# Lightning attention and a SiLU feed-forward on one core: half of block 4's first product in seven products, another order of the opening, other transfer times in the planner

## The chip, the cores and the metric

One core of a Trainium2 chip. The metric is device time in microseconds (us) of one launch, on the slowest (here the only) core. The engines are PE (TensorE, matrix products), ACT (ScalarE), DVE (VectorE), POOL (GpSimd) and SP (SyncE), which here only issues transfers. Each engine runs its own instructions in the order of the program; between engines there are semaphores.

## The reference

Attention in blocks of 64 positions with a decay per head, for 4 batches, 8 heads, 768 positions, 64 wide; then a feed-forward layer over the 3072 tokens of width 512, with 2048 hidden features.

```python
for b in range(nb):                       # 12 blocks of 64
    qb, kb, vb = (q[:, :, sl], k[:, :, sl], v[:, :, sl])
    intra = np.einsum('bhic,bhjc->bhij', qb, kb) * Dmask[None]
    intra = np.einsum('bhij,bhjd->bhid', intra, vb)
    inter = np.einsum('bhid,bhde->bhie', qb * lam_pow[None], kv_state)
    out[:, :, sl] = intra + inter
    kb_dec = kb * rev_pow[None]
    kv_state = lam_block[None, :, None, None] * kv_state + np.einsum('bhsd,bhse->bhde', kb_dec, vb)
...
h = x @ w_in                              # x: (3072, 512), w_in: (512, 2048)
g = h * (1.0 / (1.0 + np.exp(-h)))
return (g @ w_out).astype(np.float32)     # w_out: (2048, 512)
```

Inputs and output are float32. The kernel multiplies in bfloat16 and sums in float32.

## The kernel before

**Units and sets.** A unit is 128 positions of one batch (24 units). Two units form a set, for which q, k and v are loaded together (512 KB each): sets 0 to 3 hold the first two units of one batch each ("paired", `prepare_2`, `first_2`, `second_2`), sets 4 to 11 hold the same unit of two batches. The feed-forward works on eight groups: groups 0 to 3 of 256 tokens (a paired set each) and groups 4 to 7 of 512 tokens (two sets each). Blocks here are numbered by unit: block 4 is group 6, the last but one, and group 7 is the last.

**Attention of a set.** The names are those of the tiles in the profile. `kq`: keys cast to bfloat16 (ACT or DVE) and queries scaled by powers of the decay (DVE). `tr`: PE transposes of `kq`, copied to `kqT`; from set 5 on a DMA does this. `vd`: scaled values. `st_ps` holds the scores, masked by DVE into `st`. `d_ps` holds the products of keys and values, from which DVE makes the running states `y`, `xf` (float32) and ACT or POOL the block-diagonal bfloat16 copies `xe`. `x_ps` gets the two products `vd` x `st` (`outs`) and state x queries (`inter`), and is copied to `xt`, the transposed input of the feed-forward.

**Feed-forward.** `product1` multiplies `xt` by `w_in`: four products for each `h_ps` result, then SiLU on ACT into `g`. In a group of 512 tokens it has 16 results of 4 products with 512 columns. For group 7, `product1_spared` does this in seven products in place of eight (Strassen's scheme in Winograd's form): sums of the quarters of `w_in` (`S1` to `S4`, tile `wsum`) and of `xt` (`T1` to `T4`, tile `xsum`) are made by DVE, and in four parts (`jp`) two PSUM banks `P` and `R` take the seven products, with copies (`m`, `h_ps`) and sums (`h`) by ACT and DVE between them. The second product, by `w_out` into `o_ps`, is plain for the first eight units (`product2_plain`, four steps of four products with 512 columns, a quarter of `w_out` each) and in seven products for the rest (`product2`, `products_of`, with sums `s`).

**Order.** Nothing runs in the order in which it is written. Each piece of work is a `Task` with a key, the engines that may do it with an estimated cost, what it depends on, and the buffers that it takes from counted pools. `Planner.order` goes through time with these costs and a model of the transfers (`SMALL`, `WIDE`, `LARGE`, `HALF` and others: bytes of a packet and two times; `FIRST`: time from issue to first packet), gives each free engine the ready task with the smallest key, and so fixes for each engine one order, in which the program is then written. Its times have no part in the run; on the chip only the order and the semaphores count. Where PE has nothing to do in the first 24 us of the plan, dummy products (`ones`) are put in.

**Transfers.** Loads of q, k and v are issued by SP, weights by POOL, results by ACT and at the end by SP. `SEQUENCE` gives the order of the loads; a mark such as `@1.2` makes the issuing engine wait until an earlier load has landed, by a copy to `gate` of one element of it:

```python
SEQUENCE = "s0 i0@0.2 s1 i1a@0.2 i1b i2 i3 o0 o1 s2@1.2 o2 o3 s3 s4"
```

So set 2's loads wait for set 1's values, and the third and fourth quarter of `w_out` (`o2`, `o3`) for set 2's keys. Sets 0 to 3 load queries, keys, values in this order.

**Lines of the profile.** L513 and L693 `tr`; L588 and L737 scores; L534 and L727 states; L614, L619, L759, L767 `x_ps`; L905 `product1`, L917 its SiLU; L1023 the seven products of the last group, L1047 their SiLU; L940 plain second product, L1153 that in seven; L1236 dummies; L342 and L344 copies by ACT and DVE; L349 every DVE operation with two tensors; L360 gates of POOL; L380 and L385 loads by SP; L406 and L409 weights.

Of the kernel before, what the change touches and what calls it, by code (L numbers as in the profile page):

```python
# [33 lines left out]

SMALL, WIDE, CAST, LARGE, HALF, TURN = (256, 17.5, 20.0), (512, 25.0, 28.0), (256, 14.0, 31.0), (2048, 88.0, 90.0), (1024, 58.0, 58.0), (1024, 50.0, 50.0)


class Planner:
# [5 lines left out]
    BIAS = {"DVE": 0.2}  # L44
    SLOW, SLOWER = 15.5, 1.8
    DENSE, THIN, REST = (9.6, 17.0), 24.0, 0.3
    FIRST, LAST, AHEAD = {"SP": 1.9, "ACT": 1.15, "POOL": 2.5}, 1.0, 0.75

# [168 lines left out]
def kernel(  # L217
# [30 lines left out]
                 xt2=2, xt4=2, g=18, s=12, m=3, osb=3, one=3, two=8, att=6, sp=2)  # L248
    BY_POOL, IN_BY_POOL, PLAIN, SPARED = (), (), 8, 1
    CASTING, SUMS_AFTER, HURRY, SUMS_ON, HOLD, ONTO = 12, 16, 0.0, 9.0, 1, 24  # L250
    EARLY, PACE = 1.0, 1.0
    OPEN, FILLED, SCALED = 4, True, ()
    QUERIES = (0, 1, 2, 3)
    SCORED, SOON, VD_ON, HALVED = (0, 1), 3, {"DVE": 0.7}, 0
    EAGER, CALM, ON = 8.0, 1.0, 6.0
# [92 lines left out]
    def tt(e, o, a, b, op):  # L348
        (nc.vector if e == "DVE" else nc.gpsimd).tensor_tensor(o, a, b, op=op)  # L349


    gate = const.tile([128, 16], F32, name="gate")
# [49 lines left out]
    def load_w(key, what, j, part):  # L402
        def go(e):
            if what == "i":
                cs = {"": slice(512 * j, 512 * j + 512), "a": slice(512 * j, 512 * j + 256), "b": slice(512 * j + 256, 512 * j + 512)}[part]
                nc.gpsimd.dma_start(out=w_in_bf[:, :, cs], in_=w_in_r[:, :, cs])  # L406
            else:
                ks = slice(4 * j, 4 * j + 4)
                nc.gpsimd.dma_start(out=w_out_bf[:, ks, :], in_=w_out_r[:, ks, :])  # L409

        t = pool_task(add((key, 0), {"POOL": 0.8}, go, [], [], 0.5243 if part else 1.0486,
                          HALF if part else LARGE, prior=pool_last[-1:], late=1.0))
        wload.setdefault((what, j), []).append(t)
        for h in ("a", "b") if not part else part:
            wload[what, j, h] = t
# [64 lines left out]
    def prepare_2(o, rs, lk, lq, lv):  # L480
# [5 lines left out]
        def cast(e, i, a):  # L486
            src = rs[i].tile[:, :, a, :].rearrange("p (m h) d -> p m h d", h=2)
            if i:
                rate = lam_q2[:, :, a].rearrange("p (m h) -> p m h", h=2)
                tt(e, o.kq_of()[:, i, :, a], src, rate[:, :, :, None].to_broadcast([128, NP, 2, 64]), AL.mult)  # L490
            else:
                copy(e, o.kq_of()[:, i, :, a], src)

        o.ck = [[add((s - (2.95 if i and o.si in SCALED else 1.0), i), {"DVE": 0.7} if i else {"DVE": 0.45, "ACT": 0.63}, lambda e, i=i, a=a: cast(e, i, a),
                     deps=(lk, lq)[i], bufs=[rs[i], o.kq]) for a in range(2)] for i in range(2)]
        after("k", [t for ts in o.ck for t in ts])

        def scale_v(e, a):
            hs = slice(4 * a, 4 * a + 4)
            tt(e, o.vd_of()[:, hs].rearrange("p h e d -> p (h e) d"), rs[2].tile[:, hs].rearrange("p h e d -> p (h e) d"),  # L500
               lam_v2[:, hs].rearrange("p h e -> p (h e)")[:, :, None].to_broadcast([128, 8, 64]), AL.mult)

        o.cv = [add((s - 0.8, 0), VD_ON, lambda e, a=a: scale_v(e, a), deps=lv, bufs=[rs[2], o.vd]) for a in range(2)]
        after("v", o.cv)
# [18 lines left out]
    def first_2(o):  # L523
# [42 lines left out]
        def rest():  # L566
            td = add((s - 0.6, 0), {"PE": 0.45}, states, deps=o.cv + o.ck[0], bufs=d_ps + [o.kq, o.vd])
            after("b", td)
            t0 = add((s - 0.9, SOON), {"DVE": 0.42}, lambda e: tt(e, small(xf), d_ps[0].tile, rate, AL.mult), deps=[td], bufs=[d_ps[0], xf])
            o.xe_ready = blocks(o.xe_in, 0, lambda: xf.tile, t0, xf)  # L570
            t1 = add((s - 0.9, 4), {"DVE": 0.42}, lambda e: tt(e, small(y), d_ps[1].tile, xf.tile, AL.add), deps=[td, t0],
                     bufs=[d_ps[1], xf, y])
            t2 = add((s - 0.9, 5), {"DVE": 0.42}, lambda e: tt(e, xf_of(), y.tile, rate, AL.mult), deps=[t1], bufs=[y, xf_n])
            xf_t.append(t2)
            xe_t.extend(blocks(xe_n, b0 % 2, xf_of, t2, xf_n))

        if o.si not in SCORED:
            rest()
        deps = [t for t in o.turned]
        o.masked = []  # L580
        for g in range(2):
# [8 lines left out]

            ts = add((s - 0.5, g), {"PE": 0.4}, scores, deps=deps, bufs=st_ps[g] + [o.kqT])
            after("b", ts)
# [41 lines left out]
    def prepare(si):  # L634
# [28 lines left out]
        def cast(e, j, i):  # L663
            src = rs[i].tile[:, j * H:j * H + H, :]
            dst = kq_of()[:, i, j].rearrange("p m h d -> p (m h) d")
            if i:
                tt(e, dst, src, lam_q[:, :, None].to_broadcast([128, H, 64]), AL.mult)
            else:
                copy(e, dst, src)

        ck = [[add((s - 1.0, i), {"DVE": 0.7} if i else {"DVE": 0.45, "ACT": 0.63}, lambda e, j=j, i=i: cast(e, j, i),
                   deps=(lk, lq)[i], bufs=[rs[i], o.kq]) for i in range(2)] for j in range(nb)]
        if si < CASTING:
            after("k", [t for ts in ck for t in ts])

        def scale_v(e, j):
            tt(e, vd_of()[:, j], rs[2].tile[:, j * H:j * H + H, :], lam_v[:, :, None].to_broadcast([128, H, 64]), AL.mult)

        cv = [add((s - 0.8, 0), VD_ON, lambda e, j=j: scale_v(e, j),
                  deps=lv, bufs=[rs[2], o.vd]) for j in range(nb)]  # L680
# [206 lines left out]

    def product1(gi):

# [3 lines left out]
        mine = []  # L893
        for m0 in range(0, KO, 2 * per):
            g = Buf("g")
# [58 lines left out]
    W = {}  # L954
# [9 lines left out]
    def sums_of_w_in():  # L964
        bufs = {name: Buf("kq") if i else Buf("rb") for i, name in enumerate(("S1", "S2", "S3", "S4"))}
        for name, b in bufs.items():
            W[name] = lambda b=b: tile_of(b, [128, 2, 1024], BF16, "wsum")
        loads = [t for i in range(4) for t in wload["i", i]]
        done = {"A11": loads, "A12": loads, "A22": loads}

        every = [t for o in infos if rank[o.n, o.bs[0]] < SUMS_AFTER for t in o.cv] + [t for o in infos[:CASTING] for ts in o.ck for t in ts]

        def total(name, a, b, op, deps, on):
            done[name] = [add((on, 8), {"POOL": 2.4} if name in IN_BY_POOL else {"DVE": 0.7}, lambda e, ks=ks: tt(
                e, W[name]()[:, ks], W[a]()[:, ks], W[b]()[:, ks], op), deps=deps, bufs=[bufs[name]])
                          for ks in (0, 1)]

        on = SUMS_ON
        total("S1", "A21", "A22", AL.add, loads + every, on)
        total("S2", "S1", "A11", AL.subtract, done["S1"], on + 0.1)  # L980
        total("S3", "A11", "A21", AL.subtract, loads + every, on + 0.2)
        total("S4", "A12", "S2", AL.subtract, done["S2"], on + 0.3)
        return bufs, done

    def product1_spared(gi, wbufs, wdone):

# [4 lines left out]
        def X(name):  # L991
            i, r = {"B11": (0, lo), "B12": (0, hi), "B21": (1, lo), "B22": (1, hi), "T1": (0, hi)}.get(name, (0, lo))
            if name in ("T2", "T4"):
                return tile_of(two, [128, 2, 2, 256], BF16, "xsum")[:, int(name == "T4")]
            if name == "T3":
                return tile_of(one, [128, 2, 256], BF16, "xsum")
            return x.tile[:, 2 * i:2 * i + 2, r]
# [7 lines left out]
        total("T2", "T3", "B11", AL.add, done["T3"], [one, two])  # L1005
        total("T1", "B12", "B11", AL.subtract, done["T3"], [])
        total("T4", "B21", "T2", AL.subtract, done["T2"], [two])
        for jp in range(4):
            P, R = Buf("bank"), Buf("bank")
            held = [P, R, Buf("sp")]  # L1010
            low, high = Buf("g"), Buf("g")
# [22 lines left out]

            narrow = {"22": Buf("vd"), "12": Buf("st")}

# [19 lines left out]
            m6 = product(2, P, "S2", "T2", False, [c1])  # L1056
            b2, c2 = keep("kqT", [m6])
            m5 = product(3, R, "S1", "T1", True, [s11])
            m7 = product(4, P, "S3", "T3", False, [c2])
            b3, c3 = keep("xf", [m7])  # L1060
            e22 = total_of("22", b3, [m5, c3])
# [148 lines left out]

    for gi in range(len(groups) - SPARED):
        product1(gi)
    for t in waits:
        t.deps += gs[0, 0][2]
        t.bufs.append(gs[0, 0][0])
        gs[0, 0][0].left += 1
    if SPARED:
        made = sums_of_w_in()
        for gi in range(len(groups) - SPARED, len(groups)):
            product1_spared(gi, *made)  # L1220
    by_rank = sorted(rank, key=rank.get)
# [51 lines left out]
```

## Time and profile before

| What | Value |
|---|---|
| Median of 3 runs (lowest to highest) | 204.62 us (204.29 to 204.93) |
| The profiled execution: its own time | 204.46 us |
| Its span, first to last instruction | 202.4 us |
| Mean granted clock of PE | 0.997 |
| Busy: PE, DVE, ACT, POOL | 188.1, 135.5, 114.2, 21.8 us |
| DMA | 33.40 MB, mean 165 GB/s |
| PE products of L905 (512 columns; 256 columns) | 184 and 256 records |
| PE products of L1023 | 112 records |

The page gives busy time by engine, the span in 40 slices of 5.06 us with the busy share in tenths, and the chain of work that ended last, followed back from the end. The timeline lists instructions in order of time, like ones merged; "[idle before <-releaser]" is the idle time of the engine ahead of the instruction and what ended it. Matmuls are pipelined: the length of one record holds its latency, so that the pace of a row of them is read from start to start, or from the lengths in the chain.

### The profile page before, as it was taken

To read this page: it belongs to the slowest core of one execution; us is meant where nothing else is said; L and a number is where in the kernel's file an instruction comes from. 1 tells how busy PE (TensorE), PEld (TensorE's weight loads), DVE (VectorE), ACT (ScalarE), POOL (GpSimd) and SP (SyncE) were. 2 spreads that over 40 slices of the span, in tenths; PEclk is the share of its full clock that TensorE was granted. 3 is DMA by queue.
4 is the path that set the end of the run, shared out by engine and by line. 5 is a ranking of instruction groups with operands and counts; after the bars stand their busy time and mean duration, and the time that the engine had idled before them with its cause. 6 is when DMAs were issued, how large, how long until landed. Compare 5 with 4: busy or idle time off the path is not lost.

```text
span 202.4 us, 5779 instructions
## 1 busy us (share of the span) xinstructions
PE 188.1 (93%) x2494; PEld 135.0 (67%) x2512; DVE 135.5 (67%) x269; ACT 114.2 (56%) x207; POOL 21.8 (11%) x48
## 2 busy tenths in 40 slices
PE   0588999999999999999999999999999999999992
PEld 0476788557678655544488746486676778888881
DVE  6499620595997950969999774999577553646511
ACT  3836666327567642357764394945656575685320
POOL 6093100310110100001011000110200000000000
PEclk9999999999999999999999999999999999999998
DMA  3999999999999989999999999948001111003313
GB/s 94 301 274 202 216 215 250 254 193 212 239 269 242 206 204 261 174 267 212 202 142 231 253 194 222 225 104 160 2 3 55 52 52 36 19 0 107 104 50 108
DMA packets 87067, 33.40 MB, mean 165 GB/s; under 512 B 65026, under 2 KB 86018, under 8 KB 87042
## 3 DMA queue, kind: packets, MB, share of 16 engines
q1 hardware_dynamic: 77154, 23.07, 57.0%
q0 software_dynamic: 4752, 4.19, 12.9%
q10 hardware_dynamic: 5136, 5.77, 8.9%
q8 instruction: 19, 0.31, 0.7%
q14 instruction: 6, 0.05, 0.1%
HBM read 27.27 MB, written 6.29 MB: 166 GB/s over the span
## 4 chain that ended last, share of the span: by engine, by line
PE 84%; DVE 6%; DMA 4%; ACT 3%; issue 1%; DVEq 0%; SPq 0%
PE h_ps L905 33%; PE o_ps L1153 22%; PE o_ps L940 14%; PE h_ps L1023 6%; DMA raw<-in_k_dram 3%; DVE st L349 2%; PE x_ps L767 2%; PE d_ps L727 1%; PE tr L513 1%; PE x_ps L759 1%; DVE vd L349 1%; PE st_ps L737 1%; DMA out_dram<-osb 1%; ACT xt L342 1%; DVE kqT L344 1%
## 5 line engine op out<-in xcount | busy, mean ns | idle before, releaser
L905 PE MATMUL h_ps<-xt,w_in_bf 128*128 128x256 bf16 (+1 forms) x440 | 73.7, 317 | 0.7 <-ACT xt L342 0.3
L905 PEld LDWEIGHTS <-w_in_bf 128*128 128x128 bf16 x448 | 42.9, 98 | 24.9 <-issue 0.3
L917 ACT ACTIVATE g<-h_ps 128x512 bf16<-128x512 f32 x80 | 46.8, 595 | 20.9 <-PE h_ps L905 20.3
L940 PE MATMUL o_ps<-w_out_bf,g 128*128 128x512 bf16 x118 | 28.6, 379 | 0.8 <-issue 0.5
L1153 PEld LDWEIGHTS <-g 128*128 128x128 bf16 x256 | 25.0, 98 | 3.7
L349 DVE TENSOR_TENSOR st<-st_ps,tri 128x512 bf16<-128x512 f32 x32 | 20.3, 682 | 9.3 <-PE st_ps L737 9.3
L1153 PEld LDWEIGHTS <-s 128*128 128x128 bf16 x192 | 18.7, 98 | 2.8
L349 DVE TENSOR_TENSOR kq<-raw,lam_q 128x512 bf16<-128x512 f32 x24 | 16.3, 698 | 6.2 <-DMA raw<-in_q_dram 4.5
L940 PEld LDWEIGHTS <-g 128*128 128x128 bf16 x128 | 12.0, 98 | 12.0
L349 DVE TENSOR_TENSOR osb<-o_ps,m 128x512 f32<-128x512 f32 (+1 forms) x15 | 8.6, 581 | 13.4 <-ACT m L342 8.6
L342 ACT ACTIVATE xt<-x_ps 128x512 bf16<-128x512 f32 x16 | 9.7, 631 | 12.3 <-PE x_ps L767 9.2
L349 DVE TENSOR_TENSOR vd<-raw,lam_v 128x512 bf16<-128x512 f32 x24 | 15.7, 682 | 0.7 <-DMA raw<-in_v_dram 0.7
L1153 PE MATMUL o_ps<-w_out_bf,s 128*128 128x256 bf16 x128 | 15.3, 273 | 0.0
L1153 PE MATMUL o_ps<-wsum,g 128*128 128x256 bf16 x128 | 15.1, 273 | 0.0
L1153 PE MATMUL o_ps<-w_out_bf,g 128*128 128x256 bf16 x128 | 14.8, 273 | 0.0
L342 ACT ACTIVATE osb<-o_ps 128x512 f32<-128x512 f32 (+1 forms) x13 | 7.3, 564 | 12.7 <-PE o_ps L940 8.6
L349 DVE TENSOR_TENSOR s<-g 128x512 bf16<-128x512 bf16 x16 | 7.2, 447 | 10.8 <-ACT g L917 8.1
L342 ACT ACTIVATE m<-o_ps 128x512 f32<-128x512 f32 (+1 forms) x13 | 6.7, 515 | 13.1 <-PE o_ps L1153 12.9
L513 PE MATMUL tr<-ident,kq 128*128 128x128 bf16 x64 | 6.1, 241 | 7.7 <-DVE kq L349 7.5
L342 ACT ACTIVATE kq<-raw 128x512 bf16<-128x512 f32 x14 | 8.4, 624 | 4.5 <-DMA raw<-in_k_dram 4.0
L346 POOL CAST xe<-xf 64x256 bf16<-64x256 f32 (+1 forms) x8 | 5.1, 640 | 49.4 <-DVE xf L349 39.3
L513 PEld LDWEIGHTS <-kq 128*128 128x128 bf16 x64 | 4.6, 107 | 8.4 <-DVE kq L349 7.9
(90 smaller groups left out, 225.0 us busy)
## 6 DMA issues: line engine op xcount, KB each, us to landing
raw<-in_q_dram SPq DMA_DIRECT2D x12, 512.0 KB, 8.2
raw<-in_k_dram SPq DMA_DIRECT2D x12, 512.0 KB, 7.9
raw<-in_v_dram SPq DMA_DIRECT2D x12, 512.0 KB, 7.2
out_dram<-osb ACTq DMA_DIRECT2D x20, 256.0 KB, 4.2
w_out_bf<-in_moe_w_out_dram POOLq DMA_DIRECT2D x4, 512.0 KB, 14.9
w_in_bf<-in_moe_w_in_dram POOLq DMA_DIRECT2D x3, 512.0 KB, 11.7
w_in_bf<-in_moe_w_in_dram POOLq DMA_DIRECT2D x2, 256.0 KB, 8.2
out_dram<-osb ACTq DMA_DIRECT2D x4, 128.0 KB, 1.7
```

The source lines that it names most:

```text
L342: nc.scalar.activation(o, i, AF.Copy)
L344: nc.vector.tensor_copy(o, i)
L346: nc.gpsimd.tensor_copy(o, i)
L349: (nc.vector if e == "DVE" else nc.gpsimd).tensor_tensor(o, a, b, op=op)
L513: nc.tensor.transpose(t[:, m, a], o.kq_of()[:, i, m, a], ident)
L727: nc.tensor.matmul(d_of(c)[rp, j, m, :], lhsT=o.kq_of()[r, 0, j, m, p, :], rhs=o.vd_of()[r, j, 2 * m + p, :], start=j == 0 and m == 0, sto ...
L767: nc.tensor.matmul(x_of(c)[:, j, m, :], lhsT=o.xe[c].tile[:, (bs[0] + j) % 2, m, :], rhs=o.kqT_of()[:, 1, j, m, halves[c]], start=False, s ...
L905: nc.tensor.matmul(t[:, j, :], lhsT=w_in_bf[:, ko, 128 * (m1 + j):128 * (m1 + j) + 128], rhs=xt[gi].tile[:, ko, :], start=(ko == 0), stop= ...
L917: nc.scalar.activation(t[:, half * per:half * per + per], bank.tile, AF.Silu)
L940: nc.tensor.matmul(t, lhsT=g.tile[:, j, 128 * gp:128 * gp + 128], rhs=w_out_bf[:, ko, :], start=(ko == 0), stop=(ko == KO - 1))
L1023: nc.tensor.matmul(t[:, j, :], lhsT=W[w]()[:, k2, f:f + 128], rhs=X(r)[:, k2, :], start=first and j == 0 and k2 == 0, stop=True, skip_grou ...
L1153: nc.tensor.matmul(t[:, i_, :], lhsT=src(j)[:, k2, 128 * r:128 * r + 128], rhs=W[w]()[:, 2 * j + k2, :], start=first and i_ == 0 and j == ...
```

## The change

It has five parts.

- **Planner.** Other constants for the transfers (`LARGE`, a new class `PART` for the halved weight loads, `FIRST` for SP and POOL) and for PE's slow start (`SLOW`).
- **Opening.** `SCALED = (1,)`: set 1's query scaling gets a key 1.95 smaller. `FINE`: in the plan, the scores of each pair of heads depend on the two `kqT` copies of these heads alone, not on all four. `LAZY = 2.0`: the last state step of a paired set (`xf`) gets the key `s + 2.0` in place of `s - 0.9`.
- **Group 6 (block 4).** `MIXED = (0, 1)`: parts 0 and 1 of its first product, half of the results, go through `product1_spared`; the other half stays in `product1`, which takes a list of results for it. The scratch buffers for group 6 come from the pools `y`, `kq` and `yf`; `T1` gets a place of its own and no longer overwrites a part of `xt`.
- **Sums of `w_in`.** They no longer depend in the plan on all casts and value scalings (`every`), but follow SP's last load, and `S3` follows the last casts; three of them lie in `rb` buffers.
- **Places for other engines** (`by_act`, `by_rate`, `ON_ACT`). `ON_ACT` is empty, so nothing comes of them.

The order that the program then has, on PE from the first transposes of set 2 on: before, 88 products of groups 0 and 1 in all, `tr` x8 (queries), 32 products, 8 `o_ps`, 8 products, `tr` x8 (keys), 12 `o_ps`, states; after, 64 products, `tr` x8 (queries), 56 products, `tr` x8 (keys), 8 `o_ps`, 8 products, 8 `o_ps`, states. On SP and POOL the loads stand in the same order through set 3.

```diff
-SMALL, WIDE, CAST, LARGE, HALF, TURN = ..., (2048, 88.0, 90.0), (1024, 58.0, 58.0), (1024, 50.0, 50.0)
+SMALL, WIDE, CAST, LARGE, HALF, TURN, PART = ..., (2048, 86.0, 86.0), (1024, 58.0, 58.0), (1024, 50.0, 50.0), (1024, 45.0, 45.0)
...
-    SLOW, SLOWER = 15.5, 1.8
+    SLOW, SLOWER = 14.0, 1.8
...
-    FIRST, LAST, AHEAD = {"SP": 1.9, "ACT": 1.15, "POOL": 2.5}, 1.0, 0.75
+    FIRST, LAST, AHEAD = {"SP": 1.7, "ACT": 1.15, "POOL": 3.0}, 1.0, 0.75
...
-    OPEN, FILLED, SCALED = 4, True, ()
+    OPEN, FILLED, SCALED = 4, True, (1,)
...
+    LAZY, FINE = 2.0, True
+    MIXED, APART, KEPT = (0, 1), 1, "yf"
...
-                          HALF if part else LARGE, prior=pool_last[-1:], late=1.0))
+                          PART if part else LARGE, prior=pool_last[-1:], late=1.0))
...
-            t2 = add((s - 0.9, 5), {"DVE": 0.42}, lambda e: tt(e, xf_of(), y.tile, rate, AL.mult), deps=[t1], bufs=[y, xf_n])
+            t2 = add((s + LAZY, 5), {"DVE": 0.42}, lambda e: tt(e, xf_of(), y.tile, rate, AL.mult), deps=[t1], bufs=[y, xf_n])
...
-            ts = add((s - 0.5, g), {"PE": 0.4}, scores, deps=deps, bufs=st_ps[g] + [o.kqT])
+            ts = add((s - 0.5, g), {"PE": 0.4}, scores, deps=o.turned[g::2] if FINE else o.turned, bufs=st_ps[g] + [o.kqT])
...
-        for m0 in range(0, KO, 2 * per):
+        for m0 in tiles or range(0, KO, 2 * per):
...
-        bufs = {name: Buf("kq") if i else Buf("rb") for i, name in enumerate(("S1", "S2", "S3", "S4"))}
+        bufs = {name: Buf("kq" if name == "S3" else "rb") for name in ("S1", "S2", "S3", "S4")}
...
-        total("S1", "A21", "A22", AL.add, loads + every, on)
+        total("S1", "A21", "A22", AL.add, loads, on)
         total("S2", "S1", "A11", AL.subtract, done["S1"], on + 0.1)
-        total("S3", "A11", "A21", AL.subtract, loads + every, on + 0.2)
+        total("S3", "A11", "A21", AL.subtract, casts, on + 0.2)
...
-            narrow = {"22": Buf("vd"), "12": Buf("st")}
+            narrow = {"22": Buf("vd" if closing else "y"), "12": Buf("st" if closing else "y")}
...
-    for gi in range(len(groups) - SPARED):
+    for gi in range(len(groups) - 2):
         product1(gi)
...
+    made = sums_of_w_in()
+    left = [j for j in range(4) if j not in MIXED]
+    if left:
+        product1(len(groups) - 2, [m for j in left for m in (2 * j, 2 * j + 8)])
+    if MIXED:
+        product1_spared(len(groups) - 2, *made, MIXED)
+    product1_spared(len(groups) - 1, *made, range(4))
```

## The prediction

> **What bounds it now.** I read the page first (busy time, slices), then the chain of waits, then the timeline of the opening, then busy time by stage.
>
> ```profile
> PE 188.1 (93%) x2494; PEld 135.0 (67%) x2512; DVE 135.5 (67%) x269; ACT 114.2 (56%) x207; POOL 21.8 (11%) x48
> ...
> PE   0588999999999999999999999999999999999992
> ...
> DMA  3999999999999989999999999948001111003313
> ```
>
> TensorE (PE) is full from the fourth slice (about 20 us) to the end, and the DMA engines are full from the second slice to about 135 us. So the time is the moment at which PE becomes full, plus its work, plus any hole. The chain of waits says where that moment is, and what PE then does (columns: start, length, what):
>
> ```profile
> 24.32 0.04 issue
> 24.36 6.28 PE h_ps L905 x56
> 30.64 0.45 PE tr L513 x8
> 31.09 3.49 PE h_ps L905 x32
> 34.58 0.21 PE o_ps L940
> 34.79 0.05 issue
> 34.85 1.46 PE o_ps L940 x6
> 36.30 0.87 PE h_ps L905 x8
> 37.18 0.45 PE tr L513 x8
> 37.62 2.59 PE o_ps L940 x12
> ```
>
> From 24.36 on PE goes from piece to piece without a hole. Two of the pieces are fed by DMA: the transposes `tr` of set 2's queries at 30.64 and of its keys at 37.18. The timeline shows when their data came:
>
> ```profile
> 28.35 1.29 DVE L349 TENSOR_TENSOR kq<-raw,lam_q 128x512 bf16<-128x512 f32 x2 [4.47 <-DMA raw<-in_q_dram]
> ...
> 35.84 0.63 ACT L342 ACTIVATE kq<-raw 128x512 bf16<-128x512 f32 x1 [0.62 <-DMA raw<-in_k_dram]
> 35.84 0.43 DVE L344 CAST kq<-raw 128x512 bf16<-128x512 f32 x1 [4.29 <-DMA raw<-in_k_dram]
> ...
> 35.94 0.37 POOL L360 COPY gate<-raw 128x1 f32<-128x1 f32 x1 [12.25 <-DMA raw<-in_k_dram]
> ```
>
> The queries land at 28.35 and are scaled at 29.64; the keys land at 35.84 and are cast at 36.47. In the kernel before, PE comes to the two transposes 1.0 and 0.7 us after that, having 88 and then 120 + 8 + 8 products to do first. That margin is what the new order touches. Busy time by stage (columns: stretch, its length, then PE, PEld, DVE, ACT, POOL busy with counts, granted clock, DMA share, GB/s):
>
> ```profile
> 24.00:45.00 21.00, 20.53 (x249) 14.96 (x251) 8.54 (x17) 10.41 (x19) 2.39 (x5) 1.00 1.14 227
> ...
> 150.00:186.00 36.00, 35.89 (x338) 29.07 (x339) 20.41 (x46) 23.71 (x42) 0.00 (x0) 1.00 0.14 45
> ```
>
> **The opening, up to 24 us.** The products begin in earnest when set 1's `xt` is there: its ACT half is written 23.59 to 24.31. Behind it lies a DVE queue: vd x2 (10.70 to 11.98), four masks `st` (to 14.38), set 1's keys and queries, vd x2, four masks (to 21.91), three state steps, `xt`. The new DVE order is vd x2, one mask, both query scalings of set 1, three masks, y, kqT, y, kqT, vd x2, four masks. By the rows (mask 0.62 from start to start, scaling pair 1.29, the others about 0.4): 11.98 + 0.6 + 1.25 + 1.85 + 4 x 0.4 + 1.25 + 2.45 = 20.98, against 21.91. Three things pay for it: set 0's second `xt` goes to ACT (0.7), its state step `xf` goes behind set 1's masks, and the key casts no longer stand in the way. The scaling doesn't stall DVE: set 1's queries must have landed by 12.6. The transfers ahead of them and the one behind are first used at 6.25, 7.97, 9.90 and 13.38, so theirs, between the last two, was there at about 11.6. Then x_ps, eight products, the state product (0.39): set 1's `xt` at about 23.5, 0.8 earlier. Scores by pairs of heads change no wait that counts: the first scores already start at 10.61, before DVE's second kqT copy (10.36 to 10.78) is done. Dummy products fall from 32 to 28, all before 17 us, off the path.
>
> **What PE then does.** Its new order is 16, 8 and 40 products, set 2's query transposes, 56 products, its key transposes, 8 `o_ps`, 8 products. So 64 products stand ahead of the query transposes (88 before), and 8 `o_ps` and 8 products that stood ahead of the key transposes now stand behind them. The queues of SP and of POOL's loads are the same, in order, through set 3; SP's waits ahead of set 2's loads are for transfers alone; so I leave both landings where they are. Then:
> - eight products to 23.55 and 32 more at 0.109 (3.49 for 32): 27.05. The transposes must wait for 29.1 (first scaling) and 29.7 (second): a hole of 2.0 + 0.5 us, and they end at 30.1.
> - 56 products, 6.1 us: 36.2. The key transposes wait for 36.5 and end at 36.95.
> - Before had, by 37.62, also done 8 `o_ps` (1.72 with its issue time) and 8 products (0.87). The new order has that at 36.95 + 2.59 = 39.54: **1.92 us later**.
>
> The opening's 0.8 us is swallowed by the first hole, and so would be any further gain or loss there of up to 2 us. Behind these waits the in-order PE queue holds everything, and ACT and DVE wait for PE, so nothing makes up for it: before has no idle time left to give.
>
> **The next load.** POOL's gate (35.94) starts the last two quarters of w_out on the same landing. Before first uses the third quarter at 45.27. By the planner's keys the last four `o_ps` ahead of set 2's x_ps now use it: at 43.97 - 0.87 + 1.92 = 45.0. If it landed just at 45.27 that is 0.25 late; if well before, nothing. I take 0.2.
>
> **Block 4's half product.** Out go 32 products of 512 columns, in come 56 of 256. Rows of the chain: 12 of 512 in 2.59 (216 ns), 12 of L1023 in 1.31 (109 ns): 32 x 0.216 - 56 x 0.109 = **0.8 us less** PE. ACT and DVE get six copies (0.60), four sums (0.69) and four sums of `xt` (0.42): 8.0 us. In 150 to 186 DVE is busy 20.4 of 36 and ACT 23.7, so it fits in sum. The eight sums of w_in (0.68 each) come out of one lump and go between masks and `s` sums in 110 to 150, where DVE is at 23 to 27 of 30. If that cover were gone, a mask late by one such sum costs 0.7. Sums of w_out move ahead of set 3's masks too. Chains of product, copy, product run in two banks, with plain tiles between; in the existing block L1023 has 0.0 idle before it. I take 0.3 for all of this (ends: 0 and 1.0; it can't be below nothing, since PE has no idle time there to win). The tail has the same order.
>
> **Sum**, against the profiled execution (204.46 us, of it 202.4 span; the 2.1 around it stays): + 1.92 + 0.2 + 0.3 - 0.8 = + 1.6. With the median of the runs (204.62, 0.16 above the profiled one) the same sum gives 206.2; I say 206.1.
>
> **The clock after the hole.** PE runs at a slow pace at first, near half, as two rows of the same dummy product show (1.25 us and 0.83 for 12, with 0.2 of latency in both):
>
> ```profile
> 12.40 1.25 PE L1236 MATMUL ones<-ident 128*128 128x128 bf16 x12
> ...
> 16.70 0.83 PE L1236 MATMUL ones<-ident 128*128 128x128 bf16 x12
> ```
>
> After that no idle stretch of PE is over 0.4 us, and none slows it. A hole of 2.5 us in a row of 3 is shown nowhere here. If it brings the slow pace back for as long as at the start (7.0 to some 13 us), half of that is lost, 3 us; the least is nothing. I take nothing, since the row is nearer to the short gaps, and the middle for the rival. The Trainium skill ("TensorE: Matmul & The Clock Gate", Part 1) says that the clock halves after an idle window of about 3.4 us, free-running, and is back after one busy window. By that, 2.5 us can't fill a window, and if it counted all the same the loss would be an estimated 1.7 us.
>
> **Rivals.**
> 1. *The clock falls in the hole* (0.14): 1.5 us more for the 56 products, of which 0.3 is wait for the keys anyway: some 207.3. For it: the longest idle stretch of the kernel. Against: a transpose falls into it.
> 2. *The loads land sooner, and the new order is right* (faster; 0.08). The change renews the planner's transfer times, and the order fits queries landed by 25.7 (27.05 less the scaling) and keys by 33.0 (27.05 + 0.45 + 6.1 less the cast). Set 0's queries need 5.4 us from issue (0.81) to use, set 2's 12.5 (15.85 to 28.35), so it is not impossible. Then PE is full from 23.55: - 0.8 - 0.8 = 202.9. It decides if the keys land 2 us or more ahead of 35.84. Against: same queues, same full DMA engines. In between, keys sooner by 1 to 2 us (0.09): 204.0 to 205.2.
> 3. *ACT and DVE bound blocks 3 to 5* (0.10): the sums of w_in or the copies come late two or three times: 206.1 + 1 = 207.1.
> 4. *The change does little*: only if the holes were filled by other work; PE's order is fixed in the program, so this has no chance of its own.
>
> **Numbers.** Forecast 0.59 at 206.1, own range 205.4 to 206.8. The range of 204.8 to 207.8 holds it, rival 3, most of rival 1 and a part of the half-way case. 0.3% is 0.6 us, about what a measurement of this kernel can tell. Faster 0.09, within 0.09, slower 0.82.
>
> **What would show it.** In the new profile: set 1's `xt` at 23.5; in the timeline a hole of 2 to 3 us on PE ahead of the transposes at about 27, released by DVE's query scaling and the DMA behind it; the key transposes at 36.5; the chain going through `DMA raw<-in_k_dram` or in_q instead of set 0's keys; `o_ps` behind w_out at 45; L905 at 32 fewer, L1023's line at 168 products. I am wrong if set 2's queries are scaled before 27, or if PE is full through 27 to 37.

## Result, and the profile after

The changed kernel takes 207.89 us (median of 6 runs, 206.81 to 209.06), beside 204.55 us for the kernel before (6 runs, 204.29 to 204.93): a ratio of 1.0162, with a 95% interval of 1.0137 to 1.0188. It is slower, as forecast, but by 3.3 us where 1.5 had been forecast, and just outside the range. The profiled execution took 208.25 us, with a span of 206.4: 4.0 us over the span of before.

The page of the kernel after, where the lines of busy time, slices and clock answer to those of before:

```profile
PE 191.0 (93%) x2532; PEld 139.1 (67%) x2532; DVE 139.6 (68%) x280; ACT 114.9 (56%) x211; POOL 22.9 (11%) x47
...
PE   0599949999999999999999999999999999999991
...
PEclk9999996999999999999999999999999999999998
```

Two digits are new: a 4 in PE's row (sixth slice, 25.8 to 31 us), and a 6 in the row of the clock in the slice behind it. The timeline of PE shows the hole (start, length, what, and in brackets the idle time ahead and what ended it):

```profile
29.72 0.23 PE L534 MATMUL tr<-ident,kq 128*128 128x128 bf16 x1 [2.60 <-DVE kq L352]
30.32 0.56 PE L534 MATMUL tr<-ident,kq 128*128 128x128 bf16 x7 [0.37 <-DVE kq L352]
30.72 7.94 PE L932 MATMUL h_ps<-xt,w_in_bf 128*128 128x256 bf16 x56
```

Set 1's `xt` is ready at 23.4, and the products end at 27.13. Then PE waits 2.60 us for the first scaling of set 2's queries, and 0.37 for the second. The chain of waits runs through exactly this place:

```profile
15.94 13.01 DMA raw<-in_q_dram
...
28.97 1.30 DVE kq L352 x2
...
30.32 0.56 PE tr L534 x7
30.88 7.78 PE h_ps L932 x56
38.66 0.45 PE tr L534 x8
...
41.71 1.73 PE o_ps L967 x8
```

The 56 products take 7.78 us. At 109 ns each they would take 6.1. Busy time by stretches of 3.41 us tells why (columns: stretch, its length, then PE, PEld, DVE, ACT, POOL busy with counts, granted clock, DMA share, GB/s):

```profile
27.66:31.08 3.42, 0.99 (x12) 0.83 (x13) 1.45 (x3) 0.09 (x1) 0.00 (x0) 1.00 1.19 216
31.08:34.49 3.41, 3.41 (x19) 2.41 (x17) 0.27 (x1) 1.66 (x3) 0.00 (x0) 0.50 1.19 240
34.49:37.90 3.41, 3.41 (x33) 3.05 (x32) 0.43 (x1) 2.25 (x5) 1.86 (x3) 1.00 1.04 283
```

From 31.08 to 34.49 the granted clock is 0.50; before and after it is 1.00. PE was busy for 0.99 us of the stretch just ahead. In the half-clock stretch 19 PE records fall, in the next one 33.

The kernel before had done the work that ends here at 41.71 by 37.62, so PE is 4.09 us late at this point. At PE's end it is 3.37 late (202.03 against 198.66), and at the end of the span 4.0.

### The profile page after: what moved, and what is told of

Its sections match the earlier page's. It is cut to its first block, busy times and chain, and to the rows that moved or that the text cites. A ratio compares the mean times of both kernels' runs of the same rounds, so it can differ in the third digit from the quotient of the medians.

```text
span 206.4 us, 5860 instructions
## 1 busy us (share of the span) xinstructions
PE 191.0 (93%) x2532; PEld 139.1 (67%) x2532; DVE 139.6 (68%) x280; ACT 114.9 (56%) x211; POOL 22.9 (11%) x47
## 4 chain that ended last, share of the span: by engine, by line
PE 82%; DMA 11%; SPq 4%; DVE 1%; issue 0%; ACT 0%; DVEq 0%
PE h_ps L932 28%; PE o_ps L1180 22%; PE o_ps L967 14%; PE h_ps L1050 9%; DMA raw<-in_q_dram 6%; DMA raw<-in_v_dram 3%; SPq L393 3%; PE x_ps L794 2%; PE d_ps L754 1%; PE x_ps L786 1%; PE st_ps L764 1%; PE tr L534 1%; DMA out_dram<-osb 1%; DVE kq L352 1%; PE st_ps L608 1%; PE x_ps L634 1%
## 5 line engine op out<-in xcount | busy, mean ns | idle before, releaser
L932 PE MATMUL h_ps<-xt,w_in_bf 128*128 128x256 bf16 (+1 forms) x416 | 68.6, 319 | 0.0
L932 PEld LDWEIGHTS <-w_in_bf 128*128 128x128 bf16 x416 | 40.8, 100 | 22.7 <-DVE xt L347 0.2
L944 ACT ACTIVATE g<-h_ps 128x512 bf16<-128x512 f32 x72 | 42.0, 595 | 23.9 <-PE h_ps L932 23.8
L967 PE MATMUL o_ps<-w_out_bf,g 128*128 128x512 bf16 x128 | 30.8, 379 | 0.0
L345 ACT ACTIVATE m<-o_ps 128x512 f32<-128x512 f32 (+1 forms) x15 | 7.6, 509 | 17.4 <-PE o_ps L1180 17.3
L534 PE MATMUL tr<-ident,kq 128*128 128x128 bf16 x64 | 7.2, 265 | 10.8 <-DVE kq L352 10.7
L352 DVE TENSOR_TENSOR h<-h_ps,m 128x512 f32<-128x512 f32 x12 | 8.2, 687 | 8.0 <-PE h_ps L1050 4.4
L534 PEld LDWEIGHTS <-kq 128*128 128x128 bf16 x64 | 5.2, 119 | 12.1 <-DVE kq L352 11.5
L349 POOL CAST xe<-xf 64x256 bf16<-64x256 f32 (+1 forms) x8 | 7.9, 985 | 46.3 <-DVE xf L352 35.1
L345 ACT ACTIVATE kq<-raw 128x512 bf16<-128x512 f32 x15 | 9.3, 626 | 4.0 <-DMA raw<-in_k_dram 3.5
```

Of the source, the lines that this page charges most:

```text
L345: nc.scalar.activation(o, i, AF.Copy)
L349: nc.gpsimd.tensor_copy(o, i)
L534: nc.tensor.transpose(t[:, m, a], o.kq_of()[:, i, m, a], ident)
L932: nc.tensor.matmul(t[:, j, :], lhsT=w_in_bf[:, ko, 128 * (m1 + j):128 * (m1 + j) + 128], rhs=xt[gi].tile[:, ko, :], start=(ko == 0), stop= ...
L944: nc.scalar.activation(t[:, half * per:half * per + per], bank.tile, AF.Silu)
L967: nc.tensor.matmul(t, lhsT=g.tile[:, j, 128 * gp:128 * gp + 128], rhs=w_out_bf[:, ko, :], start=(ko == 0), stop=(ko == KO - 1))
```

## Experiments

All medians are of 5 to 12 runs, each set beside runs of the kernel before on the same chip (medians 204.44 to 204.58). "Hole" is PE's longest idle time after 20 us in the profile, "half" the length of the record of half clock ahead of PE's end. Experiments 4, 7 and 8 leave block 4's products plain but keep the part "Sums of `w_in`".

| Kernel | Hole, us | Half, us | PE's end, us | Median, us | Ratio to before (95%) |
|---|---|---|---|---|---|
| before | 0.26 | none | 198.66 | 204.55 | |
| after | 2.60 | 3.41 | 202.03 | 207.89 | 1.0162 (1.0137 to 1.0188) |
| 1: 40 dummies in the hole | 0.37 | none | 199.98 | 206.00 | 1.0075 (1.0058 to 1.0093) |
| 2: set 2's landings told | 2.72 | 3.41 | 202.30 | 207.70 | 1.0158 (1.0115 to 1.0200) |
| 3: old constants | 0.82 | none | 199.93 | 206.71 | 1.0106 (1.0081 to 1.0132) |
| 4: without block 4 | 2.27 | 3.42 | 201.76 | 207.26 | 1.0129 (1.0104 to 1.0155) |
| 5: block 4 alone | 0.28 | none | 198.70 | 204.62 | 0.9999 (0.9984 to 1.0015) |
| 6: constants alone | 1.94 | 3.41 | 203.20 | 209.69 | 1.0245 (1.0224 to 1.0266) |
| 7: 1 without block 4 | 0.37 | none | 200.68 | 206.10 | 1.0072 (1.0056 to 1.0087) |
| 8: opening alone | 0.82 | none | 200.57 | 205.95 | 1.0077 (1.0053 to 1.0101) |
| 9: 20 dummies | 1.32 | none | 200.65 | 205.93 | 1.0066 (1.0042 to 1.0090) |
| 10: all late landings told | 0.82 | none | 198.38 | 204.22 | 0.9981 (0.9955 to 1.0006) |
| 11: as 10, one told later | 0.82 | none | 198.44 | 204.05 | 0.9970 (0.9942 to 0.9998) |

A profile is one execution, and executions of one kernel differ: those of the kernel after lie between 206.81 and 209.06 us. The mean granted clock that comes with each execution supports the reading of the profile only in part. In the kernel after and in experiment 4, five of six executions show 0.992 or less, and the one with 1.000 is the fastest (206.81 and 206.17). In experiments 2 and 6, however, the execution with 0.999 is the slowest (209.32 and 210.01). Only the profiled execution of each kernel left a trace, so what sets the scatter stays open; the case for the clock rests on the profiles and on the medians of experiments 1 and 9.

### The hole filled: clock against wait (1 and 9)

The dummies go to the bank that the transposes then overwrite, so that the program's other instructions and their order stay:

```diff
                 t = tile_of(bank, [128, NP, 2, U], BF16, "tr")
+                for x in range(DUMMIES if (o.si, i) == (2, 1) else 0):
+                    nc.tensor.transpose(t[:, x % NP, x % 2], ident, ident)
```

> The kernel after, with 40 dummy transposes of the identity put ahead of the transposes of set 2's queries: PE is then busy (about 40 x 0.056 = 2.2 us) where the kernel after has its hole of 2.60 us; nothing else is moved. Theory (the hole costs twice: its own length, and the clock that falls behind it): the transposes still start when the queries are scaled, at about 29.7, and end at 30.3 to 30.9; the 56 products behind them take 6.1 us in place of 7.78, no record of the clock shows a half, and the time is 1.7 us below that of the kernel after, 206.2. Rival (the 56 products are slow for another reason than the clock that the hole sets, such as loads or copies that run beside them): they stay at 7.8 us and the time at 207.9.

The timeline of PE with 40 dummies:

```profile
26.70 2.40 PE L534 MATMUL tr<-ident 128*128 128x128 bf16 x40
...
29.80 0.56 PE L537 MATMUL tr<-ident,kq 128*128 128x128 bf16 x7 [0.37 <-DVE kq L353]
30.20 6.28 PE L935 MATMUL h_ps<-xt,w_in_bf 128*128 128x256 bf16 x56
```

The real transposes come no earlier than the queries allow (scaled from 28.46 on), yet the 56 products take 6.28 us where they took 7.94 in the same view of the kernel after. No half clock is recorded, and the time falls by 1.89 us to 206.00. Work that computes nothing made the kernel faster. The theory holds; the rival (something that runs beside the products) is out, since all that ran beside them is still there.

> As the kernel with 40 dummy transposes in the hole, but with 20: half of the hole is filled, 1.1 us by 20 x 0.056. Where the dummies lie, PE's idle time ahead of the first transpose of set 2's queries falls from 2.60 to about 1.4 us, with 0.37 behind it. The records of the clock so far halve it when PE is idle for 2.1 to 3.0 us of a slice of 3.41 us, that is busy for a third of it or less. Theory (it goes by the share of the slice that PE is busy, and a third is near the limit): with 1.8 us idle at most, PE is busy for 48% of any slice, the clock stays full, 56 products in 6.1 us, the time 206.0 as with 40. Rival (any gap of over a microsecond may halve the clock): 56 products in 7.3 to 7.8 us and 207.2.

With 20 dummies, first the timeline, then the stretch with the most idle time:

```profile
29.32 0.23 PE L537 MATMUL tr<-ident,kq 128*128 128x128 bf16 x1 [1.32 <-DVE kq L353]
```

```profile
27.15:30.57 3.42, 1.73 (x27) 1.40 (x24) 1.34 (x3) 0.36 (x1) 0.00 (x0) 1.00 1.19 216
```

A hole of 1.32 us, with PE busy for 1.73 us of the stretch, does nothing to the clock: a median of 205.93, the same as with 40 (the profile is that of the slowest of the six executions, 206.85). (The stretches are counted off in steps of 3.41 us from 13.50, where the full clock begins in that record.) So not every hole of over a microsecond counts. Of these 1.73 us, 1.64 are transposes, dummies and real ones: here they kept the clock full.

### Which part makes the hole (3, 6, 8)

```diff
-SMALL, WIDE, CAST, LARGE, HALF, TURN, PART = (256, 17.5, 20.0), (512, 25.0, 28.0), (256, 14.0, 31.0), (2048, 86.0, 86.0), (1024, 58.0, 58.0), (1024, 50.0, 50.0), (1024, 45.0, 45.0)
+SMALL, WIDE, CAST, LARGE, HALF, TURN, PART = (256, 17.5, 20.0), (512, 25.0, 28.0), (256, 14.0, 31.0), (2048, 88.0, 90.0), (1024, 58.0, 58.0), (1024, 50.0, 50.0), (1024, 58.0, 58.0)
-    SLOW, SLOWER = 14.0, 1.8
+    SLOW, SLOWER = 15.5, 1.8
-    FIRST, LAST, AHEAD = {"SP": 1.7, "ACT": 1.15, "POOL": 3.0}, 1.0, 0.75
+    FIRST, LAST, AHEAD = {"SP": 1.9, "ACT": 1.15, "POOL": 2.5}, 1.0, 0.75
```

> The kernel after, with the planner's old constants for transfers; opening and block 4 stay changed. The order on PE has 80 products ahead of the transposes of set 2's queries in place of 64. Theory (the new constants alone moved the transposes ahead): 16 products x 0.109 = 1.74 us of the hole are filled, a hole of 0.9 us is left, the clock stays full: 207.9 - 1.7 - 1.7 = 204.5. Rival (the opening and block 4 bring the order into disarray by themselves, whatever the constants): the time stays above 206. Second rival (a hole of 0.9 us is enough for the clock): 206.2.

The other way round, these constants put into the kernel before (the same diff with its signs turned):

> The constants alone: the kernel before with the new transfer times in the plan and nothing else; opening and block 4 as before. PE's order then has 56 products ahead of the transposes of set 2's queries in place of 88. Theory (the constants alone make the hole and with it the half clock): a hole of about 2.7 us behind these products, the products behind it at 1.2 to 1.7 us over their 6.1, and, against the kernel after without block 4 (207.26), 8 products less ahead of the hole: 0.9 more, 208.1. Rival (the constants do no harm without the new opening): 204.5.

And the opening by itself, with the old constants:

```diff
-    MIXED, APART, KEPT = (0, 1), 1, "yf"
+    MIXED, APART, KEPT = (), 1, "yf"
```

(on top of the diff of experiment 3)

> The opening alone: the kernel before with set 1's queries scaled ahead, scores by pairs of heads and the states put off, with the old constants and block 4 as before. PE's order has 80 products ahead of the transposes of set 2's queries, and no large hole is expected. Theory (the opening's 0.8 us is real only while work for PE is left to put ahead of set 2's queries and set 3's values, which land at 28.4 and 49.3 whatever PE does): no gain, 204.4 or more. By the run with the old constants and block 4 (206.7) less what block 4 saves: 207.4 at most. Rival (the opening moves all that follows it 0.8 us ahead): 203.6.

The constants alone give 209.69, 5.2 us slower, and more than expected. The timeline of PE there:

```profile
29.10 0.23 PE L513 MATMUL tr<-ident,kq 128*128 128x128 bf16 x1 [1.94 <-DVE kq L349]
29.70 0.93 PE L513 MATMUL tr<-ident,kq 128*128 128x128 bf16 x7 [0.37 <-DVE kq L349]
30.42 7.58 PE L905 MATMUL h_ps<-xt,w_in_bf 128*128 128x256 bf16 x56
```

So the new constants by themselves put the transposes ahead of their data: 56 products stand ahead of them here, and the queries land at 28.32. The median came out 1.6 us above the theory's 208.1. The profile accounts for 1.1 of this: PE's end is 1.44 later than in experiment 4, not 0.9, and the end behind it 0.6 longer; the profiled execution (209.03) is the fastest of the five. The rival, no harm from the constants, is out. Which of the constants moves the transposes was not tried.

With the old constants (experiments 3 and 8) the large hole is gone and the clock is full, but the times are 206.71 and 205.95, above the kernel before. The timeline of the opening alone shows what is late instead:

```profile
20.93 0.42 PE L634 MATMUL x_ps<-st,vd 64*64 64x128 bf16 x16 [0.32 <-DVE vd L352]
...
22.86 0.45 PE L555 MATMUL d_ps<-vd,kq 64*64 64x64 bf16 x32
...
24.44 0.38 PE L639 MATMUL x_ps<-kqT,xe 128*128 128x128 bf16 x4 [0.16 <-POOL xe L349]
25.64 2.56 PE L932 MATMUL h_ps<-xt,w_in_bf 128*128 128x256 bf16 x22 [0.82 <-DVE xt L347]
```

The same products in the kernel before:

```profile
19.70 0.44 PE L534 MATMUL d_ps<-vd,kq 64*64 64x64 bf16 x32
...
22.84 0.39 PE L619 MATMUL x_ps<-kqT,xe 128*128 128x128 bf16 x4 [0.19 <-POOL xe L346]
```

Planned with the old constants, the new keys put the scaling of set 1's values behind its masks (20.19, before at 18.23), and with it the products of keys and values (`d_ps`) and the state product later. PE waits for set 1's `xt` until 25.64, where the kernel before goes on at 24.36. The 0.8 us that the opening gains was seen only together with the new constants, and there it is lost in the hole. Alone, the opening costs 1.5 us, within its theory ("no gain", 204.4 to 207.4). Experiment 3's expectation of 204.5 missed for this reason; its first rival, that the opening brings disarray whatever the constants (above 206), is what was measured.

### The plan told the truth (2, 10, 11)

```diff
+    TOLD = {(2, 1): 3.9, (2, 0): 4.1, (2, 2): 1.0}
...
-                           kind=WIDE if n < PAIRED else SMALL, late=0.3 if si < FRESH else 3.0)])
+                           kind=WIDE if n < PAIRED else SMALL, late=TOLD.get((si, i), 0.3 if si < FRESH else 3.0))])
```

> The kernel after, with the planner told when set 2's loads really land (queries 3.9 us, keys 4.1 us, values 1.0 us later than its model has them); the rest of the change is kept. The order on PE then has 96 products ahead of the transposes of set 2's queries in place of 64. Theory (all that went wrong is the place of these transposes): no hole, no half clock, so 2.60 + 0.37 + 1.7 us come back: about 203.3, which is below the kernel before by the 0.8 us of the opening and the 0.8 us of block 4, less 0.3. Rival (the last blocks and the tail of the changed kernel cost more than was forecast, 0.6 us were seen there): 204.0. Second rival (the work of the feed-forward that is put ahead is only missing later, and PE waits there): at or above 204.6.

(A number in `TOLD` takes the place of the 0.3 that these loads had, so their planned landings move by 0.3 us less than it says.)

Here PE has no hole at 27, and reaches set 2's key transposes at 36.70 (kernel after: 38.50). But it is no faster in the end, 207.70. The second rival, waiting later, is what happened. First the timeline, then two stretches, which begin as PE runs out of other work:

```profile
50.09 0.32 PE L556 MATMUL d_ps<-vd,kq 64*64 64x64 bf16 x16 [2.72 <-DVE vd L353]
```

```profile
47.33:50.74 3.41, 0.41 (x22) 0.28 (x25) 1.29 (x2) 0.60 (x1) 0.00 (x0) 1.00 0.81 180
50.74:54.15 3.41, 3.41 (x53) 1.63 (x53) 2.06 (x5) 0.42 (x1) 0.40 (x1) 0.50 1.14 244
```

Set 3's values land at 49.32, and the plan had put their products ahead of that. It is the same pair of losses, a hole of 2.7 us and a half clock for 3.41, only 20 us later. In the kernel before, PE takes up these products at 51.12, with the values landed at 49.43 and scaled from 49.46 to 50.75: it was only 0.4 us away from this wait. So the next version tells this landing too, and those of the late quarters of w_out:

```diff
+    TOLD, HELD = {(2, 1): 3.9, (2, 0): 4.1, (2, 2): 1.0, (3, 2): 3.0}, {('o', 2): 4.0, ('o', 3): 4.0}
...
-                          PART if part else LARGE, prior=pool_last[-1:], late=1.0))
+                          PART if part else LARGE, prior=pool_last[-1:], late=HELD.get((what, j), 1.0)))
```

> As the kernel whose plan is told when set 2's loads land, with set 3's values (3.0 us) and the third and fourth quarter of w_out (3.0 us each) told as well; all parts of the change kept. That kernel waited 2.72 us for set 3's values at 47.4 and lost its clock there. Theory (opening and block 4 are worth something only where PE has other work until set 3's values land at 49.3): the largest hole is under 1 us, the clock stays full, PE's end is near that of the kernel before, 198.7, and the time 204.4 to 204.8: no gain over the kernel before, since 0.6 to 0.9 of the two parts go to shorter waits on the way and to the end. Rival (without holes the 0.8 us of the opening and the 0.8 us of block 4 are both seen): 203.0.

It takes 204.22 us: 3.7 less than the kernel after with the whole change kept, 0.2 below what the theory gave, and not to be told from the kernel before. The rival's 203.0 was not reached. PE's end is 198.38. The one hole of 0.82 us left is a wait for `xt` at 46.22.

Experiment 11 puts (3, 2) at 4.0 in place of 3.0:

> As the kernel whose plan is told the landings of set 2, of set 3's values and of the late quarters of w_out (204.22), with set 3's values told another 1.0 us later. This looks for a version below both kernels. Theory (what is left to gain is small, since set 3's values land at 49.3 whatever is done ahead): within 0.3 of it, 203.9 to 204.4, with no hole over 1 us and the clock full. Rival (PE still waits for the loads of set 3 in the run before this one): 203.5 or less.

204.05 us, as the theory had it, a ratio of 0.9970 (0.9942 to 0.9998): the lowest median here, and below the kernel before by 0.3%, only just outside the noise. Set 3's values land at 48.08 in this profile, at 49.05 in that of experiment 10, and between 48.1 and 50.4 in all profiles; so the "49.3 whatever is done" of the expectations holds only to about 1 us, and what a mere earlier landing has to do with the 0.17 us between the two medians is not known.

### Block 4 (4, 5, 7)

```diff
-    MIXED, APART, KEPT = (0, 1), 1, "yf"
+    MIXED, APART, KEPT = (), 1, "yf"
```

> The kernel after without the part for block 4 (all of its first product plain again); opening and constants stay as in the kernel after, and so do the hole and what follows it. Theory (block 4 in seven saves 0.8 us of PE and gives 0.1 back): 208.6, with PE at the last products of the last group 0.7 us later than in the kernel after. Rival (the sums and copies on DVE and ACT in blocks 3 to 5 eat it up, or hand it to the tail, where 0.6 us more were seen): 207.9 or below.

> The kernel after with the 40 dummy transposes in the hole and without the part for block 4: block 4's worth with the clock full on both sides (against the run with the dummies, 206.0). Theory (block 4 saves 0.8 us on PE and gives 0.1 back): 206.7. Rival (block 4 costs 0.6, as the runs with the half clock seem to say): 205.4.

Experiment 5 has the diff of experiment 3 and the old opening:

```diff
-    OPEN, FILLED, SCALED = 4, True, (1,)
+    OPEN, FILLED, SCALED = 4, True, ()
-    LAZY, FINE = 2.0, True
+    LAZY, FINE = -0.9, False
```

> Block 4 alone: the kernel before with the part for group 6 (half of its first product in seven, and the sums of w_in ahead of both groups), with the old opening and the old constants. PE's order is that of the kernel before up to the eighth unit's second product. Theory (block 4 saves 0.8 us of PE, 0.1 comes back, the end is as before): 203.8, faster than before. Rival (what block 4 saves is lost behind it, since the run without it was 0.6 us faster than the kernel after and not 0.8 slower): 204.4 to 205.1. Second rival (the last copies and stores end 0.6 us later, as in the kernel after): 204.4 with PE's end 0.7 earlier.

The three theories missed: 208.6, 206.7 and 203.8 were expected, and 207.26, 206.10 and 204.62 measured. Against the kernel after, taking block 4's part out made the time 0.63 us shorter (the intervals of the two ratios overlap), with PE's end 0.27 earlier. That pair is not a clean one: in experiment 4's profile the queries came earlier (hole 2.27 against 2.60) and the 56 products took 7.31 us against 7.94. From the start of the key transposes (37.62 and 38.50) to PE's end it took 164.14 and 163.53 us, so block 4 did save 0.61 of PE there. With the clock full on both sides (1 and 7) PE's end is 0.70 earlier with block 4, and the medians are 206.00 and 206.10. Experiments 3 and 8, with the old constants, are such a pair too: PE's end 0.64 earlier with block 4, and the median 0.76 higher, again with overlapping intervals. PE's saving is there; the time doesn't show it. By the profiles it is given back behind PE: from PE's end to the end of the span experiment 1 needs 4.5 us and experiment 7 needs 3.6. Of these 0.9 us some 0.35 is the last store (from DVE's last instruction to its landing 2.13 against 1.78), and 0.47 lies behind the last landing (1.81 against 1.34), where POOL's last drain is late. That block 4 is the cause of these two is not shown.

Alone (experiment 5), block 4 doesn't even end PE earlier: 198.70 against 198.66. There the chain of waits leaves PE:

```profile
139.74 1.62 DVE kq L352 x2
...
143.16 0.60 DVE wsum L352
143.76 1.20 DVE st L352 x2
...
146.38 0.44 DVE xsum L352
...
146.86 2.78 PE h_ps L1050 x24
```

From 135.96 to 146.86 the chain runs through DVE (the lines show its last 7 us): the sums of w_in stand between scalings and masks, and the first product in seven starts when the last sum of `xt` is made, with PE waiting 0.28 us for it. The kernel before has PE alone in its chain there. Part of the saving is lost here; where the rest goes, the profiles don't tell, since that run was already 0.4 us behind at 125 us, where the work is still the same.

## Why the prediction was wrong

**The step that failed is "The clock after the hole ... I take nothing".** The hole came where it was put, and its size was nearly right; behind it the clock was halved for 3.41 us. The 56 products took 1.7 us more than the 6.1 of the sum. Rival 1 had this with 0.14, at 1.5 us less 0.3. Filling the hole took 1.89 us off, to 206.00, against a forecast of 206.1.

The argument that failed was "a transpose falls into it". That does not keep the clock. The traces fit a limit on how much of a stretch of 3.41 us PE is busy: it was busy for 0.99, 1.14, 1.14 and 0.41 us in the stretch ahead of the half clock (after, experiments 4, 6 and 2), and for 1.73 us where the clock stayed full (experiment 9). The ends of the programs, where PE runs out of work, narrow it: in experiment 2 PE was busy for 1.37 us from 200.93 to 204.34, and the clock was halved behind that; in experiments 7 and 4 it was busy for 1.92 and 1.93 us of such a stretch, and the next one had full clock though PE did nothing in it. A limit on the longest idle piece in a stretch (1.94 us and more halved the clock, 1.5 us and less did not) fits the same traces; no run tells the two apart. The Trainium skill ("TensorE: Matmul & The Clock Gate", Part 1) speaks of an idle window of about 3.4 us, free-running. The traces agree with the length and that it is free-running: the full clock begins anywhere from 11.03 to 17.61 us in the profiles, and the stretches of full clock before the halving are 13.65, 17.07, 17.07 and 37.55 us long (after, experiments 4, 6 and 2), that is 4, 5, 5 and 11 times 3.41. They don't agree that the window must be idle: PE was busy for up to a third of it ahead of the half clock behind a hole, and for 40% of it at the end of experiment 2. The loss that the prediction estimated from this window, 1.7 us, is what was measured.

Point by point:
- **Opening.** Set 1's `xt` at 23.5: measured 23.4. That its gain is swallowed by the hole: right. Its gain in itself is not general; with the old constants the same keys cost 1.5 us.
- **The hole.** Forecast 2.0 + 0.5 us, until 30.1; measured 2.60 + 0.37, until 30.88. Of this 0.6 is set 2's queries landing at 28.95 in this profile, against 28.35; in the other profiles they land at 28.3 to 28.7, so this is scatter between executions, and this profile lies 0.36 above its median.
- **Keys.** Forecast a wait until 36.5. They land at 34.94, and PE, slowed, comes to them at 38.50: no wait.
- **Later by 1.92.** Measured 4.09 at 41.71: 0.78 from the end of the query transposes, 1.7 from the clock, less 0.3 for the keys' wait. With the dummies the same work ends at 39.73, 2.11 late.
- **w_out.** Forecast 0.2. The third quarter lands at 43.85 and the first `o_ps` that uses it starts at 44.04 behind other work: nothing.
- **Block 4 and the copies.** Forecast - 0.8 + 0.3. From 41.71 to PE's end - 0.72: right for the product, and the 0.3 was 0.1 in this order. Rival 3 has its place all the same: with block 4 alone, the chain runs through DVE for 11 us.
- **"The tail has the same order."** The order is the same, the length is not: span less PE's end is 4.4 us against 3.7. Nothing had been put down for this. The "2.1 around" the span, taken as fixed, was 1.85.
- **Rival 2 (loads sooner)** is out: set 2's queries land at 28.3 or later in every profile, and its keys, which were to decide it by 2 us, at 34.94 at the earliest, 0.9 ahead of 35.84.

That 206.1 and the 206.00 with full clock agree is in part luck. In experiment 1's profile 0.5 too much for w_out and blocks 3 to 5 and 0.4 too much around the span stand against 0.2 too little in the opening and 0.8 too little between PE's end and the end of the span.

## What to carry to other kernels

A wait on PE has two prices: its length, and, if it leaves PE busy for too little of a stretch of 3.41 us (1.37 us was too little here, 1.73 enough), half a stretch of work behind it (1.7 us here); so cost every new hole with both, and try dummy products in it before anything else is rebuilt. A planner's transfer time that is too early does harm in a fixed order: compare each planned landing with the trace, and correct them all, since mending one only moves PE to the next (27 to 47 us here). A saving on PE is worth its time only if nothing waits behind PE: ask what the loads allow next (set 3's values, 0.4 us away in the kernel before) and what the end of the kernel adds.

## What was not expected of the hardware

- The clock halved with PE busy for up to 1.37 us of the 3.41 us ahead, and not with 1.73. Where between these the limit lies was not tried. In the four profiles with the hole's half clock it came back after 3.41 us of full work.
- Transposes count as work for it: 1.64 of the 1.73 us that kept the clock in experiment 9.
- Behind the last store's landing, the program needs 1.32 to 1.35 us in the profiles of the kernel before and of experiments 4 to 8, 10 and 11, but 1.74 to 1.85 in the kernel after and experiments 1, 2, 3 and 9. In the kernel after, POOL's last drain ends at 205.93, while the other engines' end by 205.45. All five have the whole change or all but its constants, but so have experiments 10 and 11, with 1.33 and 1.35. What sets it stays open.
